# wo of the first 23 heads as one tile in a buffer of K and V, loaded behind the 26th K in two transfers; three gathers for the other seven heads

## The chip, the cores and the metric

One Trainium2 chip, one of its cores. The metric is the device time of one execution in microseconds (us), lower is better; the median of several runs counts. Before the change it is 1307.51 us, the median of 3 runs (1307.48 to 1307.79).

## The reference

A decode step for two batch entries with one token each: pre-LayerNorm attention over a cache of 8192 positions for 32 heads of 128, then a pre-LayerNorm MLP. All is float32.

```python
B, Sq, D = 2, 1, 512;  H, Sk, Dh = 32, 8192, 128;  F = 1792

q = (layernorm(x) @ wq).reshape(B, Sq, H, Dh).transpose(0, 2, 1, 3)
scores = einsum("bhqd,bhkd->bhqk", q, k_cache) * (Dh ** -0.5)
o = einsum("bhqk,bhkd->bhqd", softmax(scores), v_cache)
h = x + o.transpose(0, 2, 1, 3).reshape(B, Sq, H * Dh) @ wo
y = layernorm(h)
out = h + gelu(y @ w1 + b1) @ w2 + b2
```

The K cache and the V cache hold 2 x 32 x 8192 x 128 floats each, 268 MB each. wo is 4096 x 512: head h uses its rows 128 h to 128 h + 127, 0.26 MB a head.

## The kernel before

**Iterations.** The heads are taken in pairs (`QG` = 2, `NM` = 16 pairs m), and each pair for both batch entries b, so there are `NI` = 32 iterations i = 2 m + b (the loop `for i in range(NI)`). Iteration i works on one K tile and one V tile of 128 partitions x 128 positions x 128 floats: partitions 0 to 63 hold one head, 64 to 127 the other, and a partition has 64 KB in one piece of memory. A tile is 8.39 MB. Tiles lie in a pool of three buffers (`kv`, `BUFS` = 3) that K and V share in turn, behind wq, which takes the first; w1 and w2 take a buffer at the end. SyncE (SP) issues all these loads, in the order K 0, V 0, K 1, V 1 and so on (`load`, line 75), each as soon as the load three before it has been used up.

**Scores.** VectorE (DVE) multiplies the K tile in place by q in four chunks (`multiply`, L246), GpSimd (POOL) folds part of each chunk in half (`halve`, L256), and DVE sums over the head's 128 floats (`sums`, L266). When the sums of all four chunks are there, K's buffer is free. The row maximum goes through a transpose on TensorE (PE) and back (`row_max` L270/L273, `all_max` L277/L280), and ScalarE (ACT) makes the exponentials (`exps`, L286, L291).

**Values.** In iteration i + 1, before that iteration's multiplies, PE multiplies the exponentials with the V tile of iteration i (`values`, L314, 32 matmuls, which the trace shows as 64 passes). Then V's buffer is free. `total`, `inverse`, `gather` and `head_sum` (L301, L306, L320, L335) turn that into a pair's sums and one over its denominators.

**The projection by wo.** Heads 0 to 29 (`HL` = 30) go through wo while K and V are still coming; the last two are done at the end, with wo's last rows in the tile `wl`. The rows of wo for heads 0 to 29 are cut by `PLAN` into ten groups. A plain group of r rows a partition is loaded by SP from consecutive rows (line 140: 4, 4, 4, 2 and 1 rows of 2 KB a partition). A tuple is a gathered group: its numbers are the first partitions of blocks of four that are left out, and GpSimd clears the tile `wog` (L144) and gathers 8 KB into each of the 96 other partitions by an indirect DMA (L145) over a table of indices, built once at the start (L115 to L127). All groups share one buffer of the pool `wts`, so a group is loaded in the iteration after the one before it was used (`free_from`, `load_wo`). `head_out` (L350) scales a head's result and writes it in pieces into the rows `orow`; a group that a pair completes is transposed in the third chunk (`turn`, L358), copied in the fourth (`turned`, L365) and multiplied with its rows of wo into the accumulator `rowacc` (L367: one matmul a row of the partition, two passes each in the trace). These ran in iterations 4, 8, 12, 14, 18, 22, 24, 26, 28 and 30.

**The end.** After the last V the last two heads, the second LayerNorm and the MLP follow while w1 and w2 come in by six loads (L468, L472) behind V 31; the output is written at line 624.

**Order.** A scheduler orders the instructions of each engine from their dependences and their place in the program. `tc.issue_after(m)` (here `behind`) holds an instruction behind another of the same engine, and `next_of_pool` does so on GpSimd for the wo gathers and clears. `make_q` (L231) makes q for four iterations at a time and can be placed well ahead of its place in the program.

Of the kernel before, what the change touches and what calls it, by code (L numbers as in the profile page):

```python
# [9 lines left out]
F32 = mybir.dt.float32  # L10
# [3 lines left out]
ALU = mybir.AluOpType  # L14
AX = mybir.AxisListType

P = 128
# [14 lines left out]

PLAN = [4, (4, 16, 68, 72, 76, 80, 84, 88),
# [4 lines left out]
FAR = 4096  # L38
# [3 lines left out]
def tile_decode_block(ctx: ExitStack, tc: tile.TileContext, x, k, v, wq, wo, w1, b1, w2, b2, out):  # L42
# [25 lines left out]


    def load(src, i, parts):  # L70
        m, b = divmod(i, B)
        t = kv.tile([P, NS, DH], F32, name="kv", tag="kv")
        rows = src[b, QG * m:QG * m + QG].rearrange("h (p j) d -> (h p) j d", j=NS)
        for s0, n in parts:
            nc.sync.dma_start(t[:, s0:s0 + n], rows[:, s0:s0 + n])
        return t

    wqt = kv.tile([P, DC, H * DH], F32, name="wqs", tag="kv")
    nc.sync.dma_start(wqt, wq.rearrange("(p r) n -> p r n", r=DC))
# [13 lines left out]
    HL = H - QG  # L93
    groups, at = [], 0
    for blocks in PLAN:
        shut = blocks if isinstance(blocks, tuple) else None
        r = WR if shut else blocks
        n = (P - 4 * len(shut or ())) * r
        groups.append((at, n, r, shut))
        at += n  # L100
    assert at == HL * DH
    kept = [[p for p in range(P) if not any(s0 <= p < s0 + 4 for s0 in shut or ())] for _, _, _, shut in groups]
    group_end = {}
# [8 lines left out]
    for _, _, _, blocks in groups:  # L112
        if blocks and blocks not in index:
            acc = work.tile([P, 1], F32, name="ixf")
# [17 lines left out]
    wo_runs = wo.rearrange("(m r) n -> m (r n)", r=WR)  # L132
    wo_g = {}

    def load_wo(g, gate=None):
        r0, n, r, shut = groups[g]
        t = wts.tile([P, WR, D], F32, name="wog")
# [6 lines left out]
        next_of_pool(lambda: nc.gpsimd.memset(t, 0.0))  # L144
        next_of_pool(lambda: nc.gpsimd.indirect_dma_start(  # L145
            t.rearrange("p r n -> p (r n)"), None, wo_runs, bass.IndirectOffsetOnAxis(index[shut], 0),
            element_offset=r0 * D, bounds_check=n // r - 1, oob_is_err=False))
# [33 lines left out]
    otl = const.tile([P, QG, 32], F32, name="otl")  # L181
    nc.vector.memset(otl, 0.0)
    place = const.tile([B, 32], F32, name="place")
# [40 lines left out]
    def make_q(m):  # L224
        n, at = divmod(QG * m * DH, QW)
        t = psq.tile([P, 512], F32, name="qps").rearrange("p (t b d) -> p t b d", t=2, b=B)
        qps[m], qps[m + 1] = t[:, 0], t[:, 1]
# [111 lines left out]
    def head_out(h):  # L339
        r0e = 32 * (h % QG)  # L340
        rl = RL[h // QG * B + B - 1][r0e:r0e + B]
        for g, (r0, n, r, _) in enumerate(groups):
            a, end = max(r0, h * DH), min(r0 + n, (h + 1) * DH)
            while a < end:
                q = (a - r0) // r
                run = 1
                while a + run * r < end and kept[g][q + run] == kept[g][q] + run:
                    run += 1
                c0, p0 = a - h * DH, kept[g][q]
                nc.vector.tensor_scalar(orow[g % 2][:B, :r, p0:p0 + run].rearrange("b r p -> b p r"),  # L350
                                        OP[h // QG][r0e:r0e + B, c0:c0 + run * r].rearrange("b (p r) -> b p r", r=r),
                                        rl, None, op0=ALU.mult)
                a += run * r

    def turn(g):
# [3 lines left out]
        if g + 2 < len(groups) and groups[g + 2][3] and groups[g + 2][3] != groups[g][3]:  # L359
            next_of_pool(lambda: nc.gpsimd.memset(orow[g % 2][:B], 0.0))  # L360

    def turned(g):
        n = groups[g][2]
        t = work.tile([P, WR, B], F32, name="ot4")
        nc.vector.tensor_copy(t[:, :n], TP.pop(g)[:, :n])  # L365
        for r in range(n):
            nc.tensor.matmul(rowacc, t[:, r, :], wo_g[g][:, r, :], start=False,  # L367
                             stop=(g == len(groups) - 1 and r == n - 1))

    def behind(m):  # L370
        return tc.issue_after(m.ins)


# [11 lines left out]
    next_load = 0  # L385
    free_from = 1
    kt[0] = load(k, 0, cut(1))
    for i in range(NI):
        m, b = divmod(i, B)
        done = i - 1  # L390
        late = i == NI - 1
        if not late:
            if i < NI - 2:
                vt[i] = load(v, i, cut(1))
# [18 lines left out]
        if next_load < len(groups) and i == free_from:  # L413
            load_wo(next_load, MX[i - 1][:1, 0:1] if next_load == 0 else None)
            next_load += 1
            free_from = NI
        for c in range(NC):
            if i > 0 and c == 0:
                with behind(last):
                    mul = multiply(i, c)  # L420
            else:
                mul = multiply(i, c)
            ended = [g for g in group_end.get(done // B, ())] if done >= 0 and done % B == B - 1 else []
            with behind(mul):
# [17 lines left out]
            if late and c == 1:  # L442
                spare = psq.tile([P, 512], F32, name="spare", tag="qps")
                awake = stay_awake(8, ST[i][:, :NPOOL[True][0]])
            if i > 0 and c == 0:
                total(done)
            if i > 0 and c == 1 and not late:
                head_sum(done)
            if c == 2:
                for g in ended:  # L450
                    turn(g)
        sums(i, NC - 1, True)
        if b == B - 1 and m % 2 == 1 and m + 1 < NM:
            make_q(m + 1)
        if late:
# [4 lines left out]
        else:  # L460
            row_max(i)

    hl = NI - 1
    wt = kv.tile([P, 2, NS * DH // 2], F32, name="ws", tag="kv")
    w1t = wt[:, 0, :DC * F].rearrange("p (c f) -> p c f", c=DC)
# [59 lines left out]

    po2 = psq.tile([P, 512], F32, name="po2", tag="qps")[:, :P]
    hc = psm.tile([P, P], F32, name="sm")
# [123 lines left out]
```

## Time and profile before

The profiled execution has a span of 1305.9 us from its first to its last instruction; the runs shown have 1307.51 in the median, so 1.6 us lie around the span.

| | before |
|---|---|
| span of the profiled execution | 1305.9 us |
| median of the runs | 1307.51 us |
| HBM read | 562.32 MB, 431 GB/s over the span |
| DVE busy | 932.7 us (71%) |
| POOL busy | 494.2 us (38%) |
| PE busy | 446.8 us (34%) |
| ACT busy | 98.6 us (8%) |
| mean granted TensorE clock | 0.66 of full speed |

The page of the profile cuts the span into 40 equal slices and gives for each the busy share of an engine in tenths (9 is 90% or more), that of the 16 DMA engines and the GB/s that they moved. Then come the DMA queues (q1: loads that SP issues; q0: GpSimd's gathers; q8: instruction fetches) with packets, MB and their share of 16 engines' time, and the chain of waits that ended last. A row of instructions has line, engine, operation, result <- operands, shapes and count, then busy us and the mean ns of one, then the idle time before them and what ended it. A row of the timeline has its start, its length in us, engine, line, operation and count; in brackets the idle time before it. A row of the windows has the stretch and its length, the busy time and count of the engines asked for, the granted TensorE clock, the DMA share and the GB/s.

### The profile page before, as it was taken

How to read it: one execution, taken by the hardware profiler on the slowest of the kernel's cores; microseconds unless marked ns; L12 is line 12 of the kernel's file. 1: busy time of each engine (PE TensorE's matmuls, PEld its weight loads, DVE VectorE, ACT ScalarE, POOL GpSimd, SP SyncE). 2: the span in 40 equal slices, each digit the busy share in tenths (PEclk: the TensorE clock that was granted, in tenths of full speed). 3: DMA queues.
4: the chain of work that ended last, by engine and by line, in shares of the span. 5: the costliest groups of instructions: out<-in, count | busy, mean ns of one | idle time of the engine just before them, and what ended most of it. 6: DMA issues, size and time to landing. Idle time of an engine off the chain costs nothing.

```text
span 1305.9 us, 7466 instructions
## 1 busy us (share of the span) xinstructions
PE 446.8 (34%) x2934; PEld 130.9 (10%) x2934; DVE 932.7 (71%) x551; ACT 98.6 (8%) x431; POOL 494.2 (38%) x151
## 2 busy tenths in 40 slices
PE   3033313333332334413342232333323334123468
PEld 0001001010010101001010010101001011000113
DVE  3666688757688666787766787666787667797891
ACT  0000000000000000000000000000000000004440
POOL 0433344532344432444332454333444433453330
PEclk9566556766566666656766566666666666566689
DMA  9999999999999999999999999999999999999998
GB/s 418 426 440 428 438 422 444 424 440 426 442 426 440 428 438 428 426 444 430 436 426 438 430 434 436 424 442 424 440 426 432 438 432 436 429 428 429 428 434 351
DMA packets 12727, 561.50 MB, mean 430 GB/s; under 512 B 1568, under 2 KB 1584, under 8 KB 2484
## 3 DMA queue, kind: packets, MB, share of 16 engines
q1 hardware_dynamic: 11968, 557.08, 98.8%
q0 software_dynamic: 720, 3.93, 0.7%
q8 instruction: 23, 0.38, 0.1%
q14 instruction: 12, 0.10, 0.0%
q10 hardware_dynamic: 4, 0.00, 0.0%
HBM read 562.32 MB, written 0.00 MB: 431 GB/s over the span
## 4 chain that ended last, share of the span: by engine, by line
DMA 43%; DVE 24%; issue 14%; PE 12%; POOL 5%; ACT 1%; SPq 0%; POOLq 0%; DVEq 0%
DMA kv<-in_A_k_cache_dram 38%; DVE kv L246 14%; PE so L314 10%; DVE s L266 9%; POOL kv L256 5%; DMA kv<-in_A_v_cache_dram 3%; DMA ws<-in_B_w_dram 1%; ACT pt L291 1%; PE rowacc L367 1%; DVE orow L350 1%; PE sm L280 1%; PE sm L273 0%; DVE gm L277 0%; DVE mx L270 0%; ACT nb L286 0%
## 5 line engine op out<-in xcount | busy, mean ns | idle before, releaser
L246 DVE TENSOR_TENSOR kv<-kv,qps 128x4096 f32<-128x4096 f32 x128 | 562.4, 4415 | 313.8 <-DMA kv<-in_A_k_cache_dram 313.6
L256 POOL TENSOR_TENSOR kv<-kv 128x2048 f32<-128x2048 f32 (+3 forms) x128 | 476.8, 3734 | 754.1 <-DVE kv L246 566.3
L266 DVE TENSOR_REDUCE s<-kv 128x32 f32<-128x2048 f32 (+5 forms) x160 | 325.3, 2066 | 10.9 <-POOL kv L256 10.6
L314 PE MATMUL so<-kv,pt 128*8 128x512 f32 x2048 | 280.8, 709 | 42.7 <-ACT pt L291 37.3
L273 PE MATMUL sm<-ident,mx 128*1 128x128 f32 x32 | 10.9, 340 | 446.0 <-DVE mx L270 446.0
L314 PEld LDWEIGHTS so<-kv,pt 128*8 128x8 f32 x2048 | 56.4, 101 | 239.5 <-issue 194.3
L367 PE MATMUL rowacc<-wog,ot 128*2 128x512 f32 x70 | 50.3, 881 | 64.8 <-DVE ot L365 33.4
L286 ACT ACTIVATE nb<-sm 128x2 f32<-128x2 f32 x32 | 5.5, 172 | 851.4 <-PE sm L280 851.4
L231 PE MATMUL qps<-q,pick 2*64 2x256 f32 x64 | 13.8, 577 | 127.6 <-DVE kv L246 127.6
L273 PEld LDWEIGHTS sm<-ident,mx 128*1 128x1 f32 x32 | 2.5, 79 | 472.5 <-issue 278.0
L358 PE MATMUL sm<-ident,orow 2*128 2x2 f32 x35 | 5.2, 244 | 130.1 <-DVE orow L350 130.1
L320 ACT ACTIVATE ss<-so 128x512 f32<-128x512 f32 x31 | 18.5, 598 | 269.6 <-PE so L314 269.6
L260 ACT ACTIVATE kv<-kv 128x128 f32<-128x128 f32 x114 | 33.5, 295 | 24.2 <-DVE kv L246 21.4
L335 PE MATMUL sm<-ss,selr 128*34 128x128 f32 x240 | 28.7, 273 | 0.0
L291 ACT ACTIVATE pt<-s,nb 64x128 f32<-64x128 f32 x64 | 25.5, 399 | 1.4
L335 PEld LDWEIGHTS sm<-ss,selr 128*34 128x34 f32 x240 | 25.1, 112 | 0.0
L260 ACT ACTIVATION_READ_ACCUMULATOR kv<-kv 128x1 f32 x114 | 21.3, 186 | 0.0
L280 PE MATMUL sm<-gm,ones 1*128 1x2 f32 x64 | 16.6, 326 | 11.9 <-DVE gm L277 11.9
L277 DVE TENSOR_REDUCE gm<-sm 1x2 f32<-1x128 f32 x32 | 8.9, 279 | 16.2 <-PE sm L273 16.2
L231 PEld LDWEIGHTS qps<-q,pick 2*64 2x64 f32 x64 | 5.5, 192 | 136.9 <-DVE kv L246 133.2
L358 PEld LDWEIGHTS sm<-ident,orow 2*128 2x128 f32 x35 | 4.4, 207 | 132.6 <-DVE orow L350 79.9
L367 PEld LDWEIGHTS rowacc<-wog,ot 128*2 128x2 f32 x70 | 6.8, 107 | 97.9 <-issue 64.1
(110 smaller groups left out, 169.2 us busy)
## 6 DMA issues: line engine op xcount, KB each, us to landing
kv<-in_A_k_cache_dram SPq DMA_DIRECT2D x4, 4096.0 KB, 32.9
ws<-in_B_w_dram SPq DMA_DIRECT2D x3, 1792.0 KB, 18.5
kv<-in_A_v_cache_dram SPq DMA_DIRECT2D x1, 4096.0 KB, 33.4
wog<-in_A_wo_dram SPq DMA_DIRECT2D x3, 1024.0 KB
kv<-in_A_v_cache_dram SPq DMA_DIRECT2D x1, 2048.0 KB, 37.9
kv<-in_A_v_cache_dram SPq DMA_DIRECT2D x1, 1536.0 KB, 41.2
ws<-in_B_w_dram SPq DMA_DIRECT2D x1, 1024.0 KB, 17.0
wog<-in_A_wo_dram SPq DMA_DIRECT2D x1, 512.0 KB
```

The source lines that it names most:

```text
L231: nc.tensor.matmul(t[e * HP:(e + 1) * HP, :, b], pick[32 * n:32 * n + B, b, :], rows[:, :, e], start=True, stop=True)
L246: return nc.vector.tensor_tensor(kc, kc, qb, op=ALU.mult)
L256: nc.gpsimd.tensor_tensor(t[:, :, :DH // 2], t[:, :, :DH // 2], t[:, :, DH // 2:], op=ALU.add)
L260: nc.scalar.activation(kt[i][:, j, :], kt[i][:, j, :], AF.Copy, accum_out=ST[i][:, j:j + 1])
L266: nc.vector.tensor_reduce(ST[i][:, a:e], kt[i][:, a:e, :d], axis=AX.X, op=ALU.add)
L273: nc.tensor.transpose(MT[i], mx, ident)
L280: GI[i] = nc.tensor.matmul(GM[i], ones[:1, :], gm, start=True, stop=True)
L291: nc.scalar.activation(ptz[i % 2][ps, :, 4 * e:4 * e + 4], s[ps], AF.Exp, bias=nb[ps, e:e + 1], scale=SCALE, accum_out=LT[m][ps, 32 * e + ...
L314: m = nc.tensor.matmul(so[32 * n:32 * n + 4 * QG], ptz[i % 2][:, u, :], vt[i][:, 4 * u:4 * u + 4, :], start=(u < NG), stop=(u >= NS // 4 - ...
L320: return nc.scalar.activation(SS[i], so2[i % 2], AF.Copy)
L335: nc.tensor.matmul(OP[m], sel_row[:, j, B - 1 - c:B - 1 - c + QR], SS[i - 1 + c][:, j * DH:(j + 1) * DH], start=(c == 0 and j == 0), stop= ...
L367: nc.tensor.matmul(rowacc, t[:, r, :], wo_g[g][:, r, :], start=False, stop=(g == len(groups) - 1 and r == n - 1))
```

## The change

The first 23 heads of wo become one tile `wow` in one of the three buffers of K and V: 12 heads as 12 rows of 2 KB a partition (24 KB in one piece), 11 heads as 11 rows. It is loaded in iteration `XI` = 25 by two transfers from SP, in the place that V 25 had, that is behind K 25, the 26th K; V 25, K 26, V 26 and the later loads follow. All K, V and `wow` loads are now chained in program order on SP (`next_of_sp`), and the three buffers are three tags taken in strict turn (`kv_tile`).

The scaled results of the 23 heads are collected in rows of one tile, `oflat` (one DVE instruction a head, in the buffer of the gathered groups), transposed in the third chunk of iteration 24 (`turn_flat`, 23 transposes), copied in its fourth into a view of `otl`, and multiplied with `wow` in iteration 25 behind the values of V 24 (`first_heads`, 23 matmuls). The row maximum of that iteration is put behind them.

The other seven heads are three gathers of 76, 76 and 72 partitions, loaded in iterations 25, 27 and 29 and used in 26, 28 and 30. The plain groups are gone. Some orders are now fixed by `behind_all`: a multiply behind the reciprocal or the head pieces of the chunk before, `row_max` behind the copies or matmuls of that iteration, and `make_q` moves into the third chunk, behind the values.

```diff
+FLAT = (12, 11)
+NW = sum(FLAT)
-PLAN = [4, (4, 16, 68, 72, 76, 80, 84, 88),
-        4, (12, 36, 100, 104, 108, 112, 116, 120),
-        4, (8, 12, 20, 24, 68, 72, 76, 80),
-        2, (44, 52, 56, 100, 104, 108, 112, 116),
-        1, (12, 20, 24, 52, 56, 84, 88, 120)]
+PLAN = [(44, 52, 56, 72, 76, 80, 84, 88, 104, 108, 112, 116, 120),
+        (20, 24, 44, 52, 56, 68, 72, 100, 104, 108, 112, 116, 120),
+        (4, 12, 36, 40, 44, 48, 52, 56, 100, 104, 108, 112, 116, 120)]
...
+    def next_of_sp(t, rows):
+        with behind_all(sp_last[:]):
+            sp_last[0] = nc.sync.dma_start(t, rows)
+
+    def kv_tile(shape, name):
+        taken[0] += 1
+        return kv.tile(shape, F32, name=name, tag=f"kv{(taken[0] - 1) % BUFS}", bufs=1)
+
     def load(src, i, parts):
...
-            nc.sync.dma_start(t[:, s0:s0 + n], rows[:, s0:s0 + n])
+            next_of_sp(t[:, s0:s0 + n], rows[:, s0:s0 + n])
...
-    groups, at = [], 0
+    groups, at = [], NW * DH
...
+    oflat = wts.tile([P, max(FLAT) * DH], F32, name="oflat", tag="wog")
+    flat_at = [(32 * f, sum(FLAT[:f]), n) for f, n in enumerate(FLAT)]
...
-        if not shut:
-            nc.sync.dma_start(t[:, :r], wo[r0:r0 + n, :].rearrange("(p r) n -> p r n", r=r))
-            return
...
+    oT = otl.rearrange("p e r -> p (e r)")[:, :NW * B].rearrange("p (r b) -> p r b", b=B)
...
     def head_out(h):
...
+        if h < NW:
+            p0, h0 = next((p0, h0) for p0, h0, n in flat_at if h < h0 + n)
+            return nc.vector.tensor_scalar(oflat[p0:p0 + B, (h - h0) * DH:(h - h0 + 1) * DH],
+                                           OP[h // QG][r0e:r0e + B], rl, None, op0=ALU.mult)
...
+    def turn_flat():
+        turned = []
+        for p0, h0, n in flat_at:
+            t = psm.tile([P, n, B], F32, name="sm")
+            rows = oflat[p0:p0 + B, :n * DH].rearrange("b (p r) -> b r p", r=n)
+            for r in range(n):
+                nc.tensor.transpose(t[:, r, :], rows[:, r, :], ident[p0:p0 + B, p0:p0 + B])
+            turned.append((t, h0, n))
+        return turned
+
+    def first_heads():
+        for r in range(NW):
+            m = nc.tensor.matmul(rowacc, oT[:, r, :], wow[:, r, :], start=False, stop=False)
+        return m
...
-    free_from = 1
+    XI = (NW + 1) // QG * B + 1
+    free_from = XI
...
         if not late:
-            if i < NI - 2:
+            if i == XI:
+                wow = kv_tile([P, NW, D], "wow")
+                for _, h0, n in flat_at:
+                    next_of_sp(wow[:, h0:h0 + n], wo[h0 * DH:(h0 + n) * DH, :].rearrange("(p r) n -> p r n", r=n))
+            elif i < NI - 2:
+                if i == XI + 1:
+                    kt[i] = load(k, i, cut(1))
                 vt[i] = load(v, i, cut(1))
...
-                values(done)
-        if i < NI - 1:
+                valued = values(done)
+        if i == XI:
+            vt[i] = load(v, i, cut(1))
+            with behind(valued):
+                sent = [first_heads()]
+        elif i < NI - 1:
             kt[i + 1] = load(k, i + 1, parts_of.get(i + 1, cut(1)))
...
+        first = [last] if i > 0 else []
         for c in range(NC):
-            if i > 0 and c == 0:
-                with behind(last):
-                    mul = multiply(i, c)
-            else:
+            with behind_all(first):
                 mul = multiply(i, c)
+            first = []
...
                 if i > 0 and c == 1:
-                    inverse(done)
+                    first = [inverse(done)]
                 if i > 0 and c == 2 and done % B == B - 1:
                     for h in range(done // B * QG, done // B * QG + QG):
-                        head_out(h)
+                        first = [head_out(h)]
+                if c == 3 and i == XI + 2:
+                    nc.vector.memset(otl, 0.0)
+                if c == 3 and i == XI - 1:
+                    sent = [nc.vector.tensor_copy(oT[:, h0:h0 + n], t) for t, h0, n in flat]
                 if c == 3:
                     for g in ended:
-                        turned(g)
+                        sent = turned(g)
                         free_from = i + 1
...
             if c == 2:
+                if i == XI - 1:
+                    flat = turn_flat()
                 for g in ended:
                     turn(g)
+                if b == B - 1 and m % 2 == 1 and m + 1 < NM:
+                    with behind(valued):
+                        make_q(m + 1)
         sums(i, NC - 1, True)
-        if b == B - 1 and m % 2 == 1 and m + 1 < NM:
-            make_q(m + 1)
...
-            row_max(i)
+            with behind_all(sent):
+                row_max(i)
```

More of the change, by code (lines that the diff above doesn't have):

```diff
@@ L1 @@
 import math
-from contextlib import ExitStack
+from contextlib import ExitStack, contextmanager
 import concourse.bass as bass
@@ L93, in tile_decode_block @@
     HL = H - QG
-    groups, at = [], 0
[L95 to L99, printed above, removed]
+    groups, at = [], NW * DH
+    for shut in PLAN:
+        n = (P - 4 * len(shut)) * WR
+        groups.append((at, n, WR, shut))
         at += n
     assert at == HL * DH
-    kept = [[p for p in range(P) if not any(s0 <= p < s0 + 4 for s0 in shut or ())] for _, _, _, shut in groups]
+    kept = [[p for p in range(P) if not any(s0 <= p < s0 + 4 for s0 in shut)] for _, _, _, shut in groups]
     group_end = {}
@@ L112, in tile_decode_block @@
     for _, _, _, blocks in groups:
-        if blocks and blocks not in index:
+        if blocks not in index:
             acc = work.tile([P, 1], F32, name="ixf")
@@ L349, in head_out @@
                 c0, p0 = a - h * DH, kept[g][q]
-                nc.vector.tensor_scalar(orow[g % 2][:B, :r, p0:p0 + run].rearrange("b r p -> b p r"),
+                last = nc.vector.tensor_scalar(orow[g % 2][:B, :r, p0:p0 + run].rearrange("b r p -> b p r"),
                                         OP[h // QG][r0e:r0e + B, c0:c0 + run * r].rearrange("b (p r) -> b p r", r=r),
@@ L353, in head_out @@
                 a += run * r
+        return last
     def turn(g):
@@ L364, in turned @@
         t = work.tile([P, WR, B], F32, name="ot4")
-        nc.vector.tensor_copy(t[:, :n], TP.pop(g)[:, :n])
+        copied = nc.vector.tensor_copy(t[:, :n], TP.pop(g)[:, :n])
         for r in range(n):
[L367 to L371, printed above, removed]
+            m = nc.tensor.matmul(rowacc, t[:, r, :], wo_g[g][:, r, :], start=False,
+                                 stop=(g == len(groups) - 1 and r == n - 1))
+        return [copied, m]
     def stay_awake(n, lhs):
```

27 lines of the change are left out of this document (19 added, 8 removed).

## The prediction

> **What bounds the kernel now.** I read the slices of the page first, then its queue rows, then the chain of waits, and only then single iterations in the timeline.
>
> ```profile
> DMA  9999999999999999999999999999999999999998
> GB/s 418 426 440 428 438 422 444 424 440 426 442 426 440 428 438 428 426 444 430 436 426 438 430 434 436 424 442 424 440 426 432 438 432 436 429 428 429 428 434 351
> DMA packets 12727, 561.50 MB, mean 430 GB/s; under 512 B 1568, under 2 KB 1584, under 8 KB 2484
> ...
> q1 hardware_dynamic: 11968, 557.08, 98.8%
> q0 software_dynamic: 720, 3.93, 0.7%
> q8 instruction: 23, 0.38, 0.1%
> ...
> DMA 43%; DVE 24%; issue 14%; PE 12%; POOL 5%; ACT 1%; SPq 0%; POOLq 0%; DVEq 0%
> ```
>
> The DMA engines are at 9 in 39 of 40 slices, the last is the tail, and the three queues add to 99.6% of the span. The chain puts only 43% on DMA, which misleads: it follows one K through its arithmetic and back to a transfer, while other transfers run beside that arithmetic. So the end is set by bytes over rate. An engine's work costs time only if it makes a transfer start late; a saved instruction saves nothing.
>
> How much room is there before a transfer starts late? The transfer list (line, count, median us from issue to landing) and one iteration say it. The iteration is that of the 26th K (`i` = 25), landing at 1028.36; I call this moment 0 below.
>
> ```profile
> wqs<-in_A_wq_dram SPq DMA_DIRECT2D x1, 22.5
> kv<-in_A_v_cache_dram SPq DMA_DIRECT2D x31, 30.6
> kv<-in_A_k_cache_dram SPq DMA_DIRECT2D x30, 38.4
> ```
> ```profile
> 1028.36 8.75 DVE L246 TENSOR_TENSOR kv<-kv,qps 128x4096 f32<-128x4096 f32 x2 [10.67 <-DMA kv<-in_A_k_cache_dram]
> ...
> 1056.37 0.33 SPq L75 DMA_DIRECT2D kv<-in_A_v_cache_dram  x1
> ...
> 1059.42 8.60 PE L314 MATMUL so<-kv,pt 128*8 128x512 f32 x64 [1.28 <-ACT pt L291]
> ...
> 1067.61 8.75 DVE L246 TENSOR_TENSOR kv<-kv,qps 128x4096 f32<-128x4096 f32 x2 [10.12 <-DMA kv<-in_A_k_cache_dram]
> ...
> 1068.09 0.33 SPq L75 DMA_DIRECT2D kv<-in_A_k_cache_dram  x1
> ```
>
> A K is done with 28.0 us after it lands (1056.37 - 1028.36); SP then issues the V that takes its buffer. The V of the step before is done with 0.5 us after the next K lands (1068.09 - 1067.61); then the next K is issued. The rate of large packets comes from the DMA view of 700 to 710, where nothing but K and V ran (packets, MB, share of 16 engines):
>
> ```profile
> q1 hardware_dynamic: 69, 4.46, 102.9%
> ```
>
> 4.46 MB in 1.029 x 10 us is 433 GB/s, so one K or V of 8.39 MB takes 19.4 us. A median V is issued 30.6 - 19.4 = 11.2 us before the queue gets to it, a K 19.0 us before. The wq load, of the same size and with nothing ahead of it, took 22.5 us: a load must be issued 3.1 us ahead of its turn or DMA idles.
>
> **The change part by part.** *Packets.* Before, five gathers of 96 rows of 8 KB (3.93 MB) and five plain loads (3.93 MB) bring wo of 30 heads, 7.86 MB. After, 23 heads (6.03 MB) come in rows of 24 and 22 KB, and three gathers bring 76, 76 and 72 rows (1.84 MB). The bytes are the same, only the packets are larger. The DMA view of 1020 to 1042 holds one gather beside K and V:
>
> ```profile
> q1 hardware_dynamic: 148, 8.65, 90.9%
> q0 software_dynamic: 143, 0.79, 8.6%
> ```
>
> The gather ran at 0.79 MB / (0.086 x 22 us) = 417 GB/s, its neighbours at 432. For 6.03 MB, 417 against 433 GB/s is 14.46 against 13.93 us. No row shows packets of 24 KB: if they go like 8 KB ones the gain is 0, like 64 KB ones 0.5. Taking the loss as one per packet, a third as many packets leave a third of it: **-0.4 us**.
>
> *Number of issues.* Ten become five. By the rows this is worth nothing, since the queue behind them never emptied. The Trainium skill, "DMA: Bandwidth & Descriptors", section "Anatomy of one DMA", gives each DMA about 2.0 us fixed beside its bytes; five fewer would be an estimate of 10 us and 1297.5. The slices at 9 speak against it here.
>
> *A third buffer borrowed.* This is the only dangerous part. The order on SP becomes K 25, wo (two parts, 12 and 11 heads), V 25, K 26, V 26, K 27, each taking the buffer of the load three before. At 433 GB/s the parts take 3.15 MB / 433 = 7.3 us and 6.7 us. From K 25 landing at 0, wo lands at 7.3 and 13.9, V 25 at 33.3, K 26 at 52.7, V 26 at 72.1.
> - wo takes the buffer of K 24, as V 25 did: 11.2 us ahead, as before.
> - V 25 takes that of V 24, done at 0.5, turn at 13.9: 13.4 us ahead.
> - K 26 takes that of K 25, done at 28.0, turn at 33.3: **5.3 us ahead** where 3.1 are needed. Margin 2.2.
> - V 26 takes wo's, so it waits for the last matmul of the 23 heads. Its turn is at 52.7, so that must end by 49.6.
> - K 27 takes that of V 25. The matmuls of V 25 queue on PE behind the 23 heads and are far from its turn at 72.1.
>
> *The 23 heads on PE.* Before, the same 35 matmuls ran in pieces; now 23 (46 passes) stand together behind the values of V 24. The timeline, the windows (length, PE busy and count, granted clock, DMA share, GB/s) and the groups give their price:
>
> ```profile
> 1091.32 6.26 PE L367 MATMUL rowacc<-wog,ot 128*2 128x512 f32 x8 [6.23 <-issue]
> ...
> 1092.12 0.13 PEld L367 LDWEIGHTS rowacc<-wog,ot 128*2 128x2 f32 x1 [0.72 <-issue]
> 1092.98 0.13 PEld L367 LDWEIGHTS rowacc<-wog,ot 128*2 128x2 f32 x1 [0.72 <-issue]
> ...
> 1097.02 0.33 SPq L75 DMA_DIRECT2D kv<-in_A_v_cache_dram  x1
> ```
> ```profile
> 1091.30:1094.40 3.10, 3.08 (x4) 0.50 0.88 381
> 1094.40:1097.50 3.10, 3.10 (x5) 0.63 0.93 402
> 933.60:936.50 2.90, 2.90 (x4) 0.54 1.10 475
> 936.50:938.50 2.00, 2.00 (x5) 1.00 0.96 401
> ```
>
> At clock 0.50 a pass starts every 0.86 us (1092.98 - 1092.12); the run of 8 that began at 933.6 was at clock 1.00 after 2.9 us, the one at 1091.3 only near its end. At clock 1.00 a pass costs 2.00 / 4.5 = 0.45 us, with one of the five counted as half. Seven slow passes, then fast ones: the 24 passes on the first part run from 7.3 to 7.3 + 6.0 + 17 x 0.45 = 21.0, the other 22 to 30.9. That is 19 us before V 26's turn of 49.6. Row maximum 25 stands behind them on PE (its DVE part is ready at 28.0), then the first multiply of K 26 on DVE, which waits for its data until 52.7 anyway: 0 us. If that cover were gone, K 26 would start about 3 us late and the V behind it would still have some 8 us of lead.
>
> *PE and DVE work moved.* The counts stay: 35 transposes become 23 in one place and 12, pieces of heads on DVE 45 to 43.
>
> ```profile
> L350 DVE TENSOR_SCALAR orow<-sm,rlr 2x128 f32<-2x128 f32 (+7 forms) x45 | 14.0, 347 | 0.3
> L358 PE MATMUL sm<-ident,orow 2*128 2x2 f32 x35 | 5.2, 244 | 130.1 <-DVE orow L350 130.1
> L365 DVE COPY ot<-sm 128x8 f32<-128x8 f32 (+2 forms) x10 | 1.6, 157 | 0.0
> ```
>
> The 23 transposes stand in the iteration of K 24, behind the head pieces and before the fourth multiply is done; an iteration with such pieces:
>
> ```profile
> 1083.26 1.13 DVE L350 TENSOR_SCALAR orow<-sm,rlr 2x48 f32<-2x48 f32 x5
> ...
> 1086.72 4.42 DVE L246 TENSOR_TENSOR kv<-kv,qps 128x4096 f32<-128x4096 f32 x1
> ```
>
> From 1084.39 to 1091.14 there are 6.75 us; the transposes take 23 x 0.244 = 5.6 us at most. If they were not hidden, the two copies (0.3 us) and the row maximum would be 1 to 2 us late; K 24 is released by its sums, so no load is. The other orders (multiplies behind the head pieces, q's matmuls earlier) are how DVE stood already: a busy iteration, with pieces, copy and a group's matmuls, released its K after 29.4 us (1097.02 - 1067.61) against 28.0. Price 0. On POOL two gathers and two clears fall away, and POOL waits for the multiplies:
>
> ```profile
> L256 POOL TENSOR_TENSOR kv<-kv 128x2048 f32<-128x2048 f32 (+3 forms) x128 | 476.8, 3734 | 754.1 <-DVE kv L246 566.3
> L144 POOL MEMSET wog<- 128x2048 f32 x5 | 9.0, 1804 | 14.3 <-PE rowacc L367 14.3
> L145 POOL DMA_INDIRECT wog<-in_A_wo_dram,ix x5 | 5.2, 1040 | 1.4 <-POOL wog L144 1.4
> ```
>
> *Which blocks are spared.* The gathers left out forty blocks of four partitions (5 x 8) and still do (13 + 13 + 14), but now all in the last seven iterations. If the blocks serve to even out the 16 DMA engines, these drift apart until then. The Trainium skill, same page, section "The descriptor swizzle", ties each block of four partitions to one engine; by its formula fourteen engines are spared as often as before, one once less and one once more, which no run here shows. No row shows the spread in mid-run. Upper bound: the shortest lead of a V seen is 9.3 us and DMA stayed at 9,
>
> ```profile
> 230.12 0.33 SPq L75 DMA_DIRECT2D kv<-in_A_v_cache_dram  x1
> ...
> 239.45 8.75 DVE L246 TENSOR_TENSOR kv<-kv,qps 128x4096 f32<-128x4096 f32 x2 [8.32 <-DMA kv<-in_A_k_cache_dram]
> ```
>
> so the spread is under 9.3 - 3.1 = 6.2. With K 26's margin of 2.2 the first engine to run dry idles between 0 and 4.0 us. I take 0: besides the gathers only the instruction fetches (q8) can set engines apart, and they are 0.1% of their time, 1.3 us on the mean.
>
> **Sum.** Span 1305.9 - 0.4 = 1305.5. The median of the runs shown, 1307.51, is 1.6 above the profiled span; with it **1307.1**.
>
> **Rivals.** *Nothing comes of it:* packets of 24 KB go like those of 8 KB, 1307.5. For: 417 and 433 GB/s are close. Against: the loss is per packet.
>
> *K 26 is late* for the engines that run ahead: up to 4.0 us, 1307.1 to 1311.1. For: it is the smallest lead of the kernel. Against: the estimate of the spread.
>
> *The 23 heads hold wo's buffer too long* (slower). If PE stays at 0.50 and the first pass waits for both parts, they run from 13.9 for 46 x 0.86 = 39.6 to 53.5; V 26 is then 53.5 - 49.6 = 3.9 us late and DMA idles that long: 1311.0. It decides from an end at 49.6. For: PE waits idle for wo and starts at 0.50, and the run at 1091.3 stayed there for 3.1 us and more. Against: each longer run reached 1.00, and the first 24 passes need only the first part.
>
> *Fixed costs were exposed* (faster). If each issue cost what the first load shows beyond its bytes, 3.1 us, five fewer give 15.5 us: 1292.0. The skill's page named above would have 10 us by an estimate of its figure. Against: a slice without an idle engine has nothing to give back. Even the whole loss, 561.5 MB at 433 GB/s being 1296.8 us, leaves little beside the tail.
>
> **How the numbers follow.** My forecast 0.66 (its own range 1306.5 to 1307.6), nothing 0.06, K 26 late 0.12, the 23 heads too long 0.13, faster 0.03. A measurement of this kernel tells about 0.2%, 2.6 us, from no change. Same: 0.66 + 0.06 + half of K 26, 0.06 = 0.78; slower: 0.13 + 0.06 = 0.19; faster 0.03. The range goes from 1306.3 to 1311.1, the bound of both late cases.
>
> **What would show it.** Right: the DMA slices stay at 9 through the iterations of K 25 to K 27; K 26 shows about 25 us from issue to landing, V 26 over 35; the group of the 23 heads ends about 31 us after K 25 lands; q0 carries 1.84 MB. Wrong: a slice under 9 near there, a V issued right behind the last matmul of the 23 heads at over 49 us, or fewer GB/s while wo's 24 KB rows pass. A wait of SP for anything that is not the load's own buffer would make the whole picture wrong.

## The result and the profile after

The changed kernel takes 1305.14 us in the median of 15 runs (1304.5 to 1305.41), the kernel before 1307.6 (15 runs, 1307.44 to 1308.12). The ratio is 0.998, its 95% interval 0.9973 to 0.9988: 2.5 us less, where 0.4 were forecast and the range began at 1306.3. The span went from 1305.9 to 1303.4 us.

From the page after: the slices, the packets and the queues.

```profile
DMA  9999999999999999999999999999999999999998
GB/s 417 420 447 421 438 430 439 428 441 421 445 425 438 428 437 429 436 433 434 435 430 439 428 441 426 443 424 445 422 447 419 440 431 436 435 433 427 432 430 358
DMA packets 12007, 561.50 MB, mean 431 GB/s; under 512 B 1488, under 2 KB 1504, under 8 KB 2148
...
q1 hardware_dynamic: 11536, 559.18, 99.2%
q0 software_dynamic: 432, 1.84, 0.3%
q8 instruction: 23, 0.38, 0.1%
```

The bytes are those of before, and the three queues again fill 99.6% of the engines' time, now of a shorter span; what moved is the mean rate, 431 for 430 GB/s. So no idle time went away, the transfers themselves became quicker. The timeline around the new step shows it nearly as it was forecast:

```profile
1002.22 0.80 SPq L87 DMA_DIRECT2D wow<-in_A_wo_dram  x2
1012.30 8.75 DVE L266 TENSOR_TENSOR kv<-kv,qps 128x4096 f32<-128x4096 f32 x2 [8.95 <-DMA kv<-in_A_k_cache_dram]
1014.37 0.33 SPq L87 DMA_DIRECT2D kv<-in_A_v_cache_dram  x1
1021.06 22.52 PE L399 MATMUL rowacc<-wow,otl 128*2 128x512 f32 x46 [6.76 <-DMA wow<-in_A_wo_dram]
1040.31 0.33 SPq L87 DMA_DIRECT2D kv<-in_A_k_cache_dram  x1
1043.62 0.33 SPq L87 DMA_DIRECT2D kv<-in_A_v_cache_dram  x1
...
1066.29 4.42 DVE L266 TENSOR_TENSOR kv<-kv,qps 128x4096 f32<-128x4096 f32 x1 [22.19 <-DMA kv<-in_A_k_cache_dram]
```

K 25 lands at 1012.30. K 26 is issued 28.0 us later and lands 26.0 us after its issue; the 23 heads end 31.3 us after the landing (1021.06 + 22.52 - 1012.30), and V 26 is issued behind them at once. K 26 lands 54.0 us after K 25, where the prediction had 52.7: the DMA view from 1012.3 to 1066.3 also holds 0.39 MB of the first gather, 0.9 us at 433 GB/s, which the prediction's order of loads leaves out.

Then where do 2.5 us come from? Two K landings far apart, with nothing but K and V between them, show it. Up to K 24 the changed kernel loads no wo. Its K 0 and K 24, in the timeline of DVE:

```profile
42.90 8.75 DVE L266 TENSOR_TENSOR kv<-kv,qps 128x4096 f32<-128x4096 f32 x2 [30.78 <-DMA kv<-in_A_k_cache_dram]
...
972.86 8.75 DVE L266 TENSOR_TENSOR kv<-kv,qps 128x4096 f32<-128x4096 f32 x2 [9.40 <-DMA kv<-in_A_k_cache_dram]
```

These are 929.96 us. The kernel before has gathers in this stretch, so its number can't be set beside it; short stretches without wo can. Three steps of a K (six loads), first before and then after:

```profile
319.47 8.76 DVE L246 TENSOR_TENSOR kv<-kv,qps 128x4096 f32<-128x4096 f32 x2 [8.27 <-DMA kv<-in_A_k_cache_dram]
...
435.66 4.42 DVE L246 TENSOR_TENSOR kv<-kv,qps 128x4096 f32<-128x4096 f32 x1 [9.54 <-DMA kv<-in_A_k_cache_dram]
```
```profile
392.07 8.75 DVE L266 TENSOR_TENSOR kv<-kv,qps 128x4096 f32<-128x4096 f32 x2 [8.66 <-DMA kv<-in_A_k_cache_dram]
...
507.85 8.75 DVE L266 TENSOR_TENSOR kv<-kv,qps 128x4096 f32<-128x4096 f32 x2 [9.36 <-DMA kv<-in_A_k_cache_dram]
```

116.19 us became 115.78, some 0.07 us less a load of 8.39 MB, although in both only K and V run ahead of these landings (the one load of wo that the kernel before issues here stands behind its K 10, the second of its two rows). Why the same transfer is quicker was the question of the experiments.

### The profile page after: what moved, and what is told of

It is laid out like the page before. It is cut to its first block, busy times and chain, and to the rows that moved or that the text cites. A ratio compares the mean times of both kernels' runs of the same rounds, so it can differ in the third digit from the quotient of the medians.

```text
span 1303.4 us, 7415 instructions
## 1 busy us (share of the span) xinstructions
PE 436.5 (33%) x2934; PEld 129.5 (10%) x2934; DVE 929.0 (71%) x524; ACT 98.6 (8%) x431; POOL 487.2 (37%) x145
## 3 DMA queue, kind: packets, MB, share of 16 engines
q0 software_dynamic: 432, 1.84, 0.3%
## 4 chain that ended last, share of the span: by engine, by line
DMA 43%; DVE 30%; PE 11%; issue 8%; POOL 6%; ACT 1%; another core or an unknown queue 1%; SPq 0%; POOLq 0%; DVEq 0%
DMA kv<-in_A_k_cache_dram 39%; DVE kv L266 16%; DVE s L286 13%; PE so L334 10%; POOL kv L276 6%; DMA kv<-in_A_v_cache_dram 3%; DMA ws<-in_B_w_dram 1%; ACT pt L311 1%; PE sm L300 1%; PE sm L293 0%; DVE mx L290 0%; DVE gm L297 0%; DVE orow L374 0%; ACT nb L306 0%
## 5 line engine op out<-in xcount | busy, mean ns | idle before, releaser
L334 PE MATMUL so<-kv,pt 128*8 128x512 f32 x2048 | 287.0, 721 | 41.3 <-ACT pt L311 36.0
L399 PE MATMUL rowacc<-wow,otl 128*2 128x512 f32 x46 | 22.5, 655 | 6.8 <-DMA wow<-in_A_wo_dram 6.8
L407 PE MATMUL rowacc<-wog,ot 128*2 128x512 f32 x24 | 16.6, 858 | 18.7 <-issue 18.7
L383 PE MATMUL sm<-ident,orow 2*128 2x2 f32 x12 | 1.7, 246 | 48.0 <-DVE orow L374 48.0
L300 PEld LDWEIGHTS sm<-gm,ones 1*128 1x128 f32 x64 | 14.8, 286 | 21.2 <-DVE gm L297 21.2
L236 PE MATMUL so<-wqs,yT 128*2 128x512 f32 x64 | 8.3, 681 | 15.5 <-DMA wqs<-in_A_wq_dram 15.5
L311 ACT ACTIVATION_READ_ACCUMULATOR pt<-s,nb 64x1 f32 x64 | 11.8, 184 | 0.0
```

The lines of the kernel that those rows point to most:

```text
L300: GI[i] = nc.tensor.matmul(GM[i], ones[:1, :], gm, start=True, stop=True)
L311: nc.scalar.activation(ptz[i % 2][ps, :, 4 * e:4 * e + 4], s[ps], AF.Exp, bias=nb[ps, e:e + 1], scale=SCALE, accum_out=LT[m][ps, 32 * e + ...
L334: m = nc.tensor.matmul(so[32 * n:32 * n + 4 * QG], ptz[i % 2][:, u, :], vt[i][:, 4 * u:4 * u + 4, :], start=(u < NG), stop=(u >= NS // 4 - ...
L399: m = nc.tensor.matmul(rowacc, oT[:, r, :], wow[:, r, :], start=False, stop=False)
L407: m = nc.tensor.matmul(rowacc, t[:, r, :], wo_g[g][:, r, :], start=False, stop=(g == len(groups) - 1 and r == n - 1))
```

## The experiments

Ratios are to the kernel before, measured on the same chip beside each run.

**First: the suspects that the change itself names.** The first theory (A, with A1 and A2 as its finer forms) was that a load of wo in mid-run leaves the K and V packets behind it slower, so that taking wo out of the first 1000 us makes them quicker. Against it stood the size of wo's packets, the choice of the spared blocks, and the gathers as such.

*e1_gather*: the changed kernel with one more gather, whose data nobody uses, in iteration 5.

```diff
+EXTRA = (0, 32, 68, 72, 76, 80, 84, 88)
+EXTRA_AT = 5
...
-    for _, _, _, blocks in groups:
+    for blocks in [shut for _, _, _, shut in groups] + [EXTRA]:
...
+        if i == EXTRA_AT:
...
+            next_of_pool(lambda: nc.gpsimd.indirect_dma_start(
+                oflat, None, wo_runs, bass.IndirectOffsetOnAxis(index[EXTRA], 0),
```

> The changed kernel plus one more gather of 96 rows of 8 KB (0.79 MB, not used) in iteration 5, blocks of four left out unevenly, as the first gather of the kernel before had it. Bytes alone: 0.79 MB at 417 GB/s = 1.9 us, 1305.1 + 1.9 = 1307.0. Theory A (in the kernel before a wo load in the middle of the run leaves K and V slower ever after: two loads in a quiet stretch take 38.74 us before and 38.64 after the change): the later 26 iterations lose 0.1 us each on top, about 2.5 us, 1309 to 1310, and K landings from iteration 7 on are 38.74 apart again. Rival B (it is the number of wo transfers and packets, each costing a little where it runs): 1307.0 to 1307.3, K landings after it 38.64 apart.

Measured: 1310.59 us (1310.37 to 1311.14), ratio 1.0022 (1.0013 to 1.0031). That is 5.4 us for 0.79 MB, whose bytes take 1.8 us at 433 GB/s. It seemed to bear A out.

*e2_small*: `wow` in six transfers of 8 or 6 KB a partition instead of two of 24 and 22 KB.

```diff
+                    for r0 in range(0, n, WR):
+                        r1 = min(r0 + WR, n)
+                        next_of_sp(wow[:, h0 + r0:h0 + r1], rows[:, r0:r1])
```

> The changed kernel with wo of the 23 heads still in its place behind the 26th K, but in six transfers with 8 KB (the last: 6 KB) a partition instead of two with 24 and 22 KB. This prices the packet size alone. My prediction's term: 0.4 us back, 1305.5. Rival B (packets and issues explain the whole 2.5 us): 1307 or more. Theory A: 1305.4 to 1305.6, and K landings before and after as in the changed kernel.

Measured: 1305.04 (1304.44 to 1305.43), ratio 0.9979 (0.997 to 0.9988). Neither the size of the packets nor four more issues can be seen.

*e3_even*: the forty left-out blocks spread evenly over the partitions instead of as the change has them.

```diff
-PLAN = [(44, 52, 56, 72, 76, 80, 84, 88, 104, 108, 112, 116, 120),
+PLAN = [(0, 4, 8, 12, 16, 20, 24, 28, 64, 68, 72, 76, 80),
```

> The changed kernel with the forty left-out blocks of the three gathers spread so that each engine (by the block-to-engine formula) is spared 2 or 3 times instead of 0 to 5 times. Sizes 76, 76, 72 as before. If the blocks even out the engines at the end, those that were spared 4 times get up to two more blocks, 8 rows of 8 KB at 0.31 us = 2.5 us: 1306.5 to 1307.6. If the choice of blocks is worth nothing: 1305.1.

Measured: 1306.64 (1306.33 to 1307.27), ratio 0.9991 (0.9982 to 1.0). The choice of blocks is worth 1.5 us, but both kernels make it.

*e4_before_plain*: the kernel before with all of wo in plain loads, so without gathers and without tables of indices.

```diff
+PLAN = [4, 4, 4, 4, 4, 4, 4, 2]
```

> The kernel before with no gathers: all 30 heads in eight plain groups from SP (4, 4, 4, 4, 4, 4, 4, 2 rows a partition), which load every engine alike. Theory A in the form that a gather or an uneven transfer leaves K and V slower: K landings in quiet stretches 38.64 apart, 1.5 to 2 us gained there and 1 to 2.5 lost at the end without spared blocks: 1306 to 1308.5. Theory A in the form that any wo load in mid-run does it: K landings 38.74 apart, 1308.5 to 1310. Rival B: K landings 38.74 apart as in the kernel before, with 1308.5 to 1310 too; the first run tells it from the second form.

Measured: 1308.73 (1308.61 to 1309.38), ratio 1.0008 (0.9999 to 1.0017). Without a single gather this program is as slow as the kernel before, so the gathers alone were not what held K and V back.

**Second: is it the load in mid-run?** *e5_gather15* is e1_gather with the gather later.

```diff
-EXTRA_AT = 5
+EXTRA_AT = 15
```

> The changed kernel with the same extra gather of 96 rows as e1_gather (1310.6), but in iteration 15 instead of 5. Theory A1 (any wo load in mid-run slows K and V from there to the end): K landings 38.64 apart until iteration 15 and 38.74 after; half of e1's loss of rate, about 1.2 us, comes back: 1309.2 to 1309.8. Theory A2 (a load disturbs K and V only while they have not yet settled, which in the changed kernel they have by about 140 us; its own gathers after 1010 us changed nothing): K landings 38.64 apart all along, 1307.5 to 1308.5 (1.9 us of bytes and up to 1 us because the extra gather spares engines unevenly).

Measured: 1310.54 (1310.37 to 1310.72), ratio 1.0021 (1.0011 to 1.0031), no less than with the gather in iteration 5. Its K 8 and K 12, in the timeline of DVE, then K 8 of the changed kernel (its K 12 is the row at 507.85 above):

```profile
353.52 8.75 DVE L268 TENSOR_TENSOR kv<-kv,qps 128x4096 f32<-128x4096 f32 x2 [9.54 <-DMA kv<-in_A_k_cache_dram]
...
508.38 8.75 DVE L268 TENSOR_TENSOR kv<-kv,qps 128x4096 f32<-128x4096 f32 x2 [9.43 <-DMA kv<-in_A_k_cache_dram]
```
```profile
353.41 8.75 DVE L266 TENSOR_TENSOR kv<-kv,qps 128x4096 f32<-128x4096 f32 x2 [9.48 <-DMA kv<-in_A_k_cache_dram]
```

These are 154.86 and 154.44 us: K and V already went slowly here, and the gather came only in iteration 15, after 600 us. An event can't slow down what comes ahead of it: A fell, and the rate had to be a property of the whole program.

*e6_tiny*: the changed kernel with a small plain load of wo (64 partitions of 2 KB) in iteration 5, and no further table.

```diff
+        if i == 5:
+            next_of_sp(oflat[P // 2:, :D], wo[:P // 2, :])
```

> The changed kernel plus one plain load from SP in iteration 5: 64 partitions of 2 KB, 0.13 MB, every engine alike, 0.3 us of bytes, not used. Theory A in any size: K landings from iteration 7 on 38.74 apart, 1307.2 to 1307.8. If it takes an uneven or a large load: 1305.4 and K landings 38.64 apart. Rival (number of transfers): 1305.4 to 1305.6.

Measured: 1305.85 (1305.45 to 1306.25), ratio 0.9986 (0.9976 to 0.9996): 0.7 us more than the changed kernel, 0.3 of it the bytes, where A in any size had 1307.2 or more.

*e7_twice*: the 23 heads' matmuls issued twice, each at half weight, to try the margin that the prediction gave them.

```diff
-        for r in range(NW):
+        for r in list(range(NW)) * 2:
...
+                    sent = [nc.vector.tensor_scalar(oT[:, h0:h0 + n], t, 0.5, None, op0=ALU.mult) for t, h0, n in flat]
```

> The changed kernel with the matmuls of the 23 heads issued twice, their left side halved so that the sum stays. In the changed kernel they run from 8.8 to 31.3 us after K 25 lands; twice they end at about 51 to 54. V 26 takes the buffer that they read, and its turn in the queue is 54.0 after that landing, 50.9 with the 3.1 us that a load needs ahead. My model of the margin: DMA idles 0.5 to 3 us, 1305.6 to 1308.2. If a late buffer is hidden in some other way: 1305.1.

Measured: 1306.11 (1305.49 to 1307.14), ratio 0.9988 (0.9978 to 0.9997). From its timeline:

```profile
1011.80 8.75 DVE L266 TENSOR_TENSOR kv<-kv,qps 128x4096 f32<-128x4096 f32 x2 [8.76 <-DMA kv<-in_A_k_cache_dram]
...
1020.82 41.39 PE L399 MATMUL rowacc<-wow,otl 128*2 128x512 f32 x92 [5.97 <-DMA wow<-in_A_wo_dram]
...
1062.25 0.33 SPq L87 DMA_DIRECT2D kv<-in_A_v_cache_dram  x1
```

V 26 is issued 50.4 us after K 25 landed, 0.8 after the 49.6 that the prediction set as its last moment, but 0.5 ahead of the 50.9 that the changed kernel's landings give (54.0 less 3.1). The kernel is 1.0 us longer. From 1055 to 1110 its queues q1 and q0 fill 98.8% of the engines' time, those of the changed kernel 99.7%, so some 0.5 us more of DMA stand idle there; where the rest arises this run doesn't tell.

*e8_before_order*: the kernel before with only the change's new orders (the chain on SP, multiplies behind head pieces and reciprocals, `row_max` behind copies and matmuls, `make_q` in the third chunk).

```diff
+            next_of_sp(t[:, s0:s0 + n], rows[:, s0:s0 + n])
...
+            if c == 2 and b == B - 1 and m % 2 == 1 and m + 1 < NM:
+                with behind(valued):
+                    make_q(m + 1)
```

> The kernel before, with only the new orders of the change: K and V chained on SP, multiplies behind the reciprocal and the head pieces, row maximum behind copy and matmuls, q's matmuls in the third chunk. Its wo groups as before. My price of these: 0, so 1307.5 to 1307.8 and K landings 38.74 apart. If the orders are what speeds up K and V: 1305.5 to 1306 and 38.64 apart.

Measured: 1307.81 (1307.66 to 1308.07), ratio 1.0001 (0.9991 to 1.0011). The orders are worth nothing.

**Third: the place of the buffers.** What do the quick programs share (the changed kernel, e2, e3, e6, e7) and the slow ones lack (before, e1, e4, e5, e8)? The number of tables of indices: three against five, four, none, four, five. A table is 4 bytes a partition, but each tile starts on a multiple of 32 bytes, so that all tiles allocated behind the constants move by 32 bytes a table. In the programs' memory plans the first of the three K and V buffers begins at byte 24128 before and at 24064 = 94 x 256 after; the buffers are 65536 bytes apart, so all three share the remainder. Four runs moved the buffers and changed no load and no work. (Small work tiles behind the buffers move with them in every run; nothing but the small input x is loaded into those.)

*f1_before_64_down*: the kernel before, 64 bytes lower.

```diff
-    epst = const.tile([P, 1], F32, name="epst")
+    eps3 = const.tile([P, 3], F32, name="eps3")
+    epst, eps2, onesd = (eps3[:, j:j + 1] for j in range(3))
```

> The kernel before with three one-column constants (the two epsilons and 1/D) kept in one small tile of three columns instead of three tiles: each tile starts on a multiple of 32 bytes, so everything allocated behind them, the K and V buffers among it, lies 64 bytes lower in every partition (from byte 24064 = 47 x 512 on, where the changed kernel has them, instead of 24128). No instruction more or less. Theory 'address' (a K or V packet takes less time where it lands on a multiple of 512 bytes; the index tables that the change removed are what moved the buffers): two loads' K landings in the quiet stretches go from some 38.72 us apart to 38.60 and the time falls by 1.9 us, to 1305.7 (1305.3 to 1306.1); what is left of the difference to the changed kernel, about 0.5, is the change itself. Rival 'program' (the rate hangs on the gathers, their number of instructions or the queue entries): nothing changes, 1307.6 and 38.72 apart.

*f2_after_64_up*: the changed kernel, only the K and V buffers (and the small work tiles behind them) 64 bytes higher.

```diff
+    wts.tile([P, 16], F32, name="pad")
```

> The changed kernel with an unused tile of 64 bytes per partition between wo's buffer and the K and V buffers, which so begin at byte 24128, as in the kernel before, where the constants and wo's buffer stay in place. Theory 'address': K landings 38.72 us apart instead of 38.60 and the time up by 1.9 us to 1307.0 (1306.6 to 1307.4), which would leave the change itself worth about 0.5. Rival 'program': 1305.1 and 38.60, as the changed kernel.

*f3_after_128_down*: the changed kernel with four small tiles fewer, so 128 bytes lower: the edit of f1, and

```diff
-    wsum = const.tile([P, QG], F32, name="wsum")
+    wsm = const.tile([P, 2 * QG], F32, name="wsm")
+    wsum, wmean = wsm[:, :QG], wsm[:, QG:]
...
-    bsum = const.tile([B, 1], F32, name="bsum")
+    bsm = const.tile([B, 2], F32, name="bsm")
+    bsum, bmean = bsm[:, 0:1], bsm[:, 1:2]
```

> The changed kernel with its small constants in fewer tiles, so that the K and V buffers begin at byte 23936, a multiple of 128 but 384 beyond one of 512. Theory 'address' in the form that 512 bytes decide: 1307.0, K landings 38.72 apart. In the form that 128 or 64 bytes on the bank's grid decide (64 alone is out, since the kernel before is on it): 1305.1 and 38.60. Rival 'program': 1305.1 and 38.60 too, so that this run speaks only if it is slower, or together with the run that moves the buffers 64 bytes up.

*f4_gather_32_down*: e1_gather with the two epsilons in one tile, so 32 bytes lower.

```diff
-    epst = const.tile([P, 1], F32, name="epst")
+    eps3 = const.tile([P, 2], F32, name="eps3")
+    epst, eps2 = (eps3[:, j:j + 1] for j in range(2))
```

> The changed kernel with the extra, unused gather of 0.79 MB in iteration 5, with the two epsilons in one tile, so that the K and V buffers lie 32 bytes lower, on byte 24064 again (the extra index table had moved them up by 32). Theory 'address': of the 5.4 us that the gather had cost, some 2.2 go back: 1308.4 (1308.0 to 1308.8), K landings 38.60 apart away from the gather, and about 3.3 us is the gather's own price, 1.8 of it its bytes at the queue's 433 GB/s. Rival 'program': 1310.6 as without the shift, 38.72 apart.

Measured, with the last two runs below; "beyond" is the place of the K and V buffers beyond a multiple of 256 bytes:

| program | beyond 0 | beyond other | lost |
|---|---|---|---|
| kernel before | f1: 1304.63 (1304.42 to 1305.08) | 64: 1307.7 | 3.1 us |
| changed kernel | 1305.14 | 64, f2: 1307.84 (1307.41 to 1308.31) | 2.7 us |
| changed kernel | 1305.14 | 128, f3: 1307.54 (1307.01 to 1307.71) | 2.4 us |
| with the extra gather | f4: 1307.12 (1306.81 to 1307.63) | 32, e1: 1310.59 | 3.5 us |
| before, plain loads | g1: 1305.92; g2: 1305.84 | 160, e4: 1308.73 | 2.8, 2.9 us |

The ratios are 0.9976 (0.9967 to 0.9986) for f1, 1.0001 (0.9992 to 1.001) for f2, 0.9998 (0.9989 to 1.0007) for f3 and 0.9995 (0.9986 to 1.0004) for f4. The theory's direction held four times, its size (1.9 us, in f4 2.2) was too small. The place of wo's buffer doesn't matter: in f2 it stays on the grid of 256 bytes and the time is lost, in g1 it stays 160 bytes off and the time is regained. K 0 and K 24 of f2, in the timeline of DVE:

```profile
42.58 8.75 DVE L267 TENSOR_TENSOR kv<-kv,qps 128x4096 f32<-128x4096 f32 x2 [30.47 <-DMA kv<-in_A_k_cache_dram]
...
973.98 8.75 DVE L267 TENSOR_TENSOR kv<-kv,qps 128x4096 f32<-128x4096 f32 x2 [9.44 <-DMA kv<-in_A_k_cache_dram]
```

931.40 us against the changed kernel's 929.96, with the same instructions and bytes: 1.4 of the 2.2 us by which the two profiled spans differ (1305.6 against 1303.4) have arisen by then. For the kernel before, K 0 (its K 25 stands in the prediction), then K 0 and K 25 of f1:

```profile
42.64 8.75 DVE L246 TENSOR_TENSOR kv<-kv,qps 128x4096 f32<-128x4096 f32 x2 [28.54 <-DMA kv<-in_A_k_cache_dram]
```
```profile
42.69 8.75 DVE L245 TENSOR_TENSOR kv<-kv,qps 128x4096 f32<-128x4096 f32 x2 [28.57 <-DMA kv<-in_A_k_cache_dram]
...
1026.15 8.75 DVE L245 TENSOR_TENSOR kv<-kv,qps 128x4096 f32<-128x4096 f32 x2 [10.39 <-DMA kv<-in_A_k_cache_dram]
```

1028.36 - 42.64 = 985.72 us became 983.46, by a shift of 64 bytes alone.

**Fourth: which grid.** *g1_plain_96_up* is e4_before_plain with an unused tile of 96 bytes behind wo's buffer (K and V at byte 24064); *g2_plain_160_down* is it with five small tiles fewer (byte 23808 = 93 x 256, no multiple of 512). First the edit of the one, then that of the other, which has f3's merged sums too:

```diff
+        if g == 0:
+            wts.tile([P, 24], F32, name="pad")
```
```diff
-    part = const.tile([P, 1], F32, name="part")
+    few = const.tile([P, 4], F32, name="few")
+    part, epst, eps2, onesd = (few[:, j:j + 1] for j in range(4))
```

> The kernel before with all of wo in plain loads (no gathers, no index tables) and an unused tile of 96 bytes behind wo's buffer, so that the K and V buffers begin at byte 24064 = 47 x 512. Without the shift this program took 1308.73. Theory 'address': some 2 to 3 us less, 1305.7 to 1306.7, two loads' K landings 38.6 apart; the gathers of the kernel before are then worth 1 to 2 us at an equal address (1304.63 was it there). Rival 'the gathers' absence and not the address held e4_before_plain back': 1308.7.

> The same program with its small constants in fewer tiles, so that the K and V buffers begin at byte 23808, 256 bytes beyond a multiple of 512. If a multiple of 256 is enough: as g1_plain_96_up, 1305.7 to 1306.7 and 38.6 apart. If it takes 512: as without any shift, 1308.3 to 1308.9 and 38.72 apart. I hold 512 likelier (0.6): the buffers 64, 32, 96 and 128 bytes off it were all alike slow, which shows no grading by the size of the grid.

Measured: 1305.92 (1305.65 to 1306.19), ratio 0.9986 (0.9977 to 0.9995), and 1305.84 (1305.6 to 1306.2), ratio 0.9986 (0.9977 to 0.9995). K 0 and K 25 of e4_before_plain, of g1_plain_96_up and of g2_plain_160_down:

```profile
41.92 8.75 DVE L242 TENSOR_TENSOR kv<-kv,qps 128x4096 f32<-128x4096 f32 x2 [34.66 <-DMA kv<-in_A_k_cache_dram]
...
1028.14 8.75 DVE L242 TENSOR_TENSOR kv<-kv,qps 128x4096 f32<-128x4096 f32 x2 [8.54 <-DMA kv<-in_A_k_cache_dram]
```
```profile
42.29 8.75 DVE L244 TENSOR_TENSOR kv<-kv,qps 128x4096 f32<-128x4096 f32 x2 [35.03 <-DMA kv<-in_A_k_cache_dram]
...
1025.87 8.75 DVE L244 TENSOR_TENSOR kv<-kv,qps 128x4096 f32<-128x4096 f32 x2 [8.27 <-DMA kv<-in_A_k_cache_dram]
```
```profile
42.31 8.75 DVE L240 TENSOR_TENSOR kv<-kv,qps 128x4096 f32<-128x4096 f32 x2 [35.05 <-DMA kv<-in_A_k_cache_dram]
...
1025.43 8.75 DVE L240 TENSOR_TENSOR kv<-kv,qps 128x4096 f32<-128x4096 f32 x2 [8.52 <-DMA kv<-in_A_k_cache_dram]
```

986.22, 983.58 and 983.12 us. My bet on 512 bytes fell: a multiple of 256 is enough, and f3, at an odd multiple of 128, shows that 128 is not. The gathers of the kernel before, at an equal place of the buffers, are worth 1305.92 - 1304.63 = 1.3 us, about as little as can be told here: the intervals of the two ratios still overlap.

## Why the prediction was wrong

**The step that failed is the one that found only wo's packets changed** ("The bytes are the same, only the packets are larger"): the sum left every K and V at 433 GB/s. The change removes two tables of indices from the constants; that moves the three K and V buffers from 64 bytes beyond a multiple of 256 onto one, and the loads into these buffers go some 0.2% faster, as K's landings show (w1 and w2 land there too, but no row prices them by themselves). This term, absent from the sum, measures -2.7 us in the changed kernel (f2) and -3.1 in the kernel before (f1). Why the chip does this no run shows. The Trainium skill states such a grid for what is read: "DMA: Bandwidth & Descriptors", section "How a descriptor splits into AXI transactions", has transactions of 256 bytes that start on multiples of 256, and a descriptor off the grid spending beats of 32 bytes on what it doesn't use. Here only the place written to moved. The grid agrees with g2 and f3; by its count the loss would grow with the offset, one beat at 32 bytes and four at 128 in the 2048 of a 64 KB packet, an estimate of 0.05 to 0.2%, while the runs show 3.5 us at 32 (with the extra gather) and, in the changed kernel, 2.7 at 64 and 2.4 at 128, so no such grading.

The signs that the prediction gave for being right did appear (slices at 9, K 26 some 25 us from issue to landing, the 23 heads' end at 31, 1.84 MB on q0). None of them looks at the rate of K and V away from the change, so they could not show this miss.

**What is left for the change itself** is the comparison at an equal place: 1307.84 against 1307.7 us at 64 beyond, 1305.14 against 1304.63 on the grid. It is worth nothing, or costs half a microsecond, which this measurement doesn't tell from nothing. The forecast of next to no difference was right for all that the edit does apart from moving the buffers, and wrong for the kernel. The lowest time of all, f1's 1304.63 us, has none of the change: three constants merged beat the kernel before, and stand 0.5 us below the changed kernel, too close to tell these two apart.

**Packets, -0.4 us:** not borne out. It charged wo's plain loads with a rate that only a gather had shown; e2_small cut the large packets again and lost nothing.

**Number of issues, 0:** right. e2_small has four more and is 0.1 us away. The rival of exposed fixed costs alone had the kernel faster, but by 15.5 us and for a reason that this run excludes.

**The borrowed buffer, 0:** right: K 26 issued at 28.0, landing 26.0 us after issue for about 25, the 23 heads' end at 31.3 for 30.9. That end is in part luck, since two misses cancel: the matmuls began at 8.8 for 7.3 and took 22.5 us for 23.6. The margin behind the rival is borne out to about a microsecond: in e7_twice, with the heads' end near it, some 0.5 us of idle DMA appear and the kernel is 1.0 us longer.

**Orders, 0:** right (e8_before_order). **Spared blocks, 0:** nothing was lost by moving them late; that they matter at all, within the bound of 0 to 4.0 us, e3_even shows with 1.5 us.

Not settled: the loss does not grow evenly. From K 8 to K 24 three pairs agree (f2 and the changed kernel 1.3 us, before and f1 1.2, e4 and g1 1.3, which is 0.2% of some 625). Ahead of that they don't: in the changed kernel and f2, K 8 still stands 310.5 and 310.6 us behind K 0, while before and f1 differ by 0.9 us there. And from the landing of K 30 to the end of the span before takes 90.6 us and f1 89.6, f2 90.9 and the changed kernel 89.9: about 1.0 us in the last 90, far more than 0.2%. The loads are cut into smaller pieces there, so a price per packet would fit, but no run tests it.

## What to carry to other kernels

Where DMA is the bound, look where the large tiles begin: a 4-byte constant ahead of them can be worth more than the edit that brought or removed it, and whoever compares two versions keeps the buffers at the same remainder of 256 bytes, or measures the shift alone. A rate that already differs ahead of the suspected event belongs to the program as a whole, and a run that only moves the event in time shows this at once.

## What the runs showed of the hardware

In programs whose loads of 64 KB a partition were written 32, 64, 128 or 160 bytes beyond a multiple of 256 in the partition, these loads ran some 0.2% slower: 2.4 to 3.5 us of some 1305 in four programs, with no growth by the distance. At 0 and at 256 bytes beyond a multiple of 512 they were alike (1305.92 and 1305.84 us). An extra gather of 0.79 MB cost, at an equal place, 1307.12 - 1305.14 = 2.0 us, its bytes at 433 GB/s being 1.8. Six transfers in place of two cost nothing measurable while the queue behind them never emptied.
